# Gated mix of sliding-window attention and a SwiGLU feed-forward: a third gate/up tile computed as block products, and the dealing of the remaining slots

## The chip, the core and the metric

The kernel runs on one core of a Trainium2 chip. A core has five engines that work side by side and wait for each other through semaphores: TensorE (PE in the profile, its weight loads PEld), VectorE (DVE), ScalarE (ACT), GpSimd (POOL), and SyncE (SP), which here only issues transfers. The metric is the device time of one launch in microseconds. Times of repeated runs of this kernel lie within 1.2 us of each other (824.19 to 825.39 us).

## The reference

With x of 2048 rows and 512 columns, everything in float32:

```python
def _A_ref(x, wqkv, wo):                      # 32 heads of 16, window 256
    qkv = (x @ wqkv).reshape(B, S, 3, H, Dh).transpose(2, 0, 3, 1, 4)
    scores = einsum("bhqd,bhkd->bhqk", q, k) * Dh ** -0.5
    mask = (i - j >= 0) & (i - j < 256)
    o = softmax(where(mask, scores, -1e9)) @ v
    return o.reshape(B, S, D) @ wo

def _B_ref(x, w_gate, w_up, w_down):          # hidden width 1792
    return (silu(x @ w_gate) * (x @ w_up)) @ w_down

g = sigmoid((x * gate_w).sum(-1, keepdims=True))
return g * _A_ref(x) + (1 - g) * _B_ref(x)
```

## The kernel before

Every float32 operand is split into a high part (a rounded copy, made on ACT) and a low part (the rest, a subtraction on DVE or POOL), and a product is three matmuls: high by high, high by low, low by high. A matmul streams 512 columns of x; the contraction of 512 is cut into four blocks of 128. So one 128 by 512 piece of `x @ w` costs 12 matmuls of 128 rows.

The hidden width is cut into NF = 14 tiles of 128. A tile f has a gate part and an up part, (f, 0) and (f, 1), each with four pieces of 512 rows of x. They are computed in one of two ways.

**Block products.** `product` (line 367) and the loop at lines 416 to 447 handle a pair of keys at once: the pairs of `PAIRS` (lines 151 and 152) are four pairs of query/key groups, then one pair (gate, up) for each tile f below NSF (line 106). The two by two scheme forms sums of weight blocks and of x blocks and takes 7 products in place of 8. Each product is 6 matmuls (line 381), for two halves `a` of x: 7 x 2 x 6 = 84 matmuls for a pair, where the plain way takes 2 x 4 x 12 = 96. ACT copies results out of PSUM (`copied`), DVE adds (`add_to`), and for a feed-forward pair `put_c` sends the eight results of 256 KB to DRAM (`raws`) through the SP queue. While one pair's products run, the next pair's weights are fetched (`pair_fetch`) and prepared (`op_a`, `op_sums`, `op_s`, `op_z`). The last pair of the list has the other branch of that loop: it fills constant rows, stacks the queries and keys of the first head group, and fetches the first plain weights.

**Slots.** The other tiles are in `UNITS` (line 107), 24 units here. `stream` (line 581) is a generator that yields one slot at a time. The first unit goes through `whole`, 48 slots of one matmul of 128 rows. The rest goes through `lanes` (line 525): a slot there is two matmuls of 64 rows each, one in the upper and one in the lower half of the array, so 12 slots finish one 128 by 512 piece. The lower half runs LAG = 18 slots behind the upper one. When a piece is finished, `copy_out` (line 508) has ACT copy it out of PSUM (the eviction, L511) and SP writes it to `raws` three ticks later. `soft` moves an eviction that would fall in the last two ticks before the values of a group to the tick of the values. After the four pieces of a unit, `prepare` (line 299) has ACT and POOL split the next weights and SP fetch the ones after them.

**The attention stage.** The heads are in G = 8 groups of four, NB = 16 blocks of 128 rows each, so the loop at line 809 has 128 steps t of four ticks `hd`. In a tick PE gets, in this order: one score block of the next group (`stage1`, L603; DVE adds the mask and takes the maximum, L605), one score block of the present group (`stage2`, L642; ACT takes the exponential, L644; POOL cuts the window's edges, L646 and L649), then so many slots as `DEAL` says (lines 805, 806, 828). Four steps make a group of 16 ticks; at its second tick the values of the four steps before it are formed (`av`, L664) and copied out (`evacuate`). This text numbers the ticks of such a group 0 to 15: ticks 0 to 3 are part 0, 4 to 7 part 1, and so on. `DEAL` gives (4, 10, 8, 8) slots for the four parts; part 0 is dealt 1, 1, 2, 0. In the last head group (the last 16 steps) it gives 8 to every part, `stage1` has nothing left, `stage2` issues two blocks in every second tick, and pieces of the next stage are begun (`tile_early`: an exponential on ACT, two DVE reciprocal chains, splits).

Each engine takes its instructions in the order of the program. PSUM has eight banks: `stage2` has two in turn (one of them is lent to the values at ticks 1 to 2), `stage1` three, the slots three. A `stage2` matmul therefore waits until the exponential of the block two before it has been read out of the same bank. Before the loop there are 64 ticks with three slots each (lines 690 to 710), in which the first group's `stage1` runs. After the loop come the down product, the output projection and the mix (line 846 on).

The slots add up as follows: 192 before the loop and 28 x 30 + 4 x 32 = 968 in it make 1160, of which the generator has 48 + 1110 = 1158.

Of the kernel before, what the change touches and what calls it, by code (L numbers as in the profile page):

```python
# [33 lines left out]
def gated_mix(ctx, tc, xT, xn, wqk, wv, wo, wgu, wd, gw, out):  # L34
# [52 lines left out]
    def run(gen, n=None):  # L87

        while n is None or n > 0:
            if next(gen, run) is run:  # L90
                break
            n = n and n - 1
# [10 lines left out]
    def weights_of(key):  # L103
        return wqk[key[1]] if key[0] == "p" else wgu[key[1], :, key[2]]

    NSF = 2
    UNITS = [("f", f, i) for f in range(NSF, NF) for i in range(2)]

    psum = ctx.enter_context(tc.tile_pool(name="psum", bufs=1, space=PSUM))
# [17 lines left out]
    def pair_fetch(keys):  # L127
        raw = wide.tile([P, 4, 2 * P], F32, name="rw")
        for i, key in enumerate(keys):
            nc.sync.dma_start(by_k(raw[:, 2 * i:2 * i + 2].rearrange("p a n -> p (a n)")), weights_of(key))  # L130
        return raw
# [19 lines left out]
    PAIRS = [(("p", g), ("p", g + 1)) for g in range(0, G, 2)]  # L151
    PAIRS += [(("f", f, 0), ("f", f, 1)) for f in range(NSF)]
    RW = {0: pair_fetch(PAIRS[0])}
# [315 lines left out]
    with ExitStack() as A:  # L469
# [121 lines left out]
        def stage1(g, qb):  # L591

            hf, b = divmod(qb, NB // 2)
            if b == 0:
                MX[g, hf] = sm.tile([P, 4, NB // 2], F32, name="mx")
            q0, k0 = qb * P, max(0, qb - 2) * P
            n = q0 + P - k0
            for hd in range(4):
                pr, j = divmod(hd, 2)
                r = slice(64 * j, 64 * j + 63)  # L600

                ps = bank("pd") if g == 0 and pr else bank("pc")
                nc.tensor.matmul(ps[:, :n], QT[g % 2][pr][r, q0:q0 + P], KT[g % 2][pr][r, k0:k0 + n],  # L603
                                 start=True, stop=True)
                mx = nc.vector.tensor_tensor_reduce(out=ps[:, :n], in0=ps[:, :n], in1=mask[:, 3 * P - n:],  # L605
                                                    scale=1.0, scalar=NEG, op0=ALU.add, op1=ALU.max,
                                                    accum_out=MX[g, hf][:, hd, b:b + 1])
                if g == 0:
                    BEHIND.append(mx)
                yield  # L610
# [191 lines left out]
            spread(4 * (16 * g + 9) + 3, 1, stack(g + 2, 0))  # L802
            spread(4 * (16 * g + 17) + 1, 1, stack(g + 2, 1))

        DEAL = [[[(hd + 1) * n // 4 - hd * n // 4 for hd in range(4)] for n in deal] for deal in ((4, 10, 8, 8), (8, 8, 8, 8))]
        DEAL[0][0] = 1, 1, 2, 0
        scores = chain(*(stage1(*divmod(b, NB)) for b in range(NB, G * NB)))
        run(scores, 1)
        for t in range(G * NB + 1):
# [7 lines left out]
            for hd in range(4):  # L817
# [9 lines left out]
                if t < G * NB:  # L827
                    run(steps, DEAL[t >= g7][part][hd])
                if hd == 1 and values:
# [205 lines left out]
```

## Time and profile before

| | us |
|---|---|
| runs: lowest, median, highest | 824.19, 825.08, 825.39 |
| the profiled execution: its time | 822.77 |
| its span, first to last instruction | 821.1 |
| block products of the six pairs (L381), first to last matmul | 53.9 to about 165 |
| slots of `lanes` (L564) | 177.9 to 616.9 |
| `stage2` (L642) | 216.8 to 616.5 |

The profile gives the busy time of each engine, the span in 40 slices, and groups of instructions by line. Its chain of waits is followed back from the last instruction to what released it. The timeline lists single instructions by start and duration; where several of one kind follow on each other it gives the time from the first start to the last end and their number. Matmuls are pipelined: a matmul of 512 columns is listed with some 0.39 us, while the next one starts about 0.22 us after it, so that starts and not durations tell the pace.

### The profile page before, as it was taken

How to read it: one execution, taken by the hardware profiler on the slowest of the kernel's cores; microseconds unless marked ns; L12 is line 12 of the kernel's file. 1: busy time of each engine (PE TensorE's matmuls, PEld its weight loads, DVE VectorE, ACT ScalarE, POOL GpSimd, SP SyncE). 2: the span in 40 equal slices, each digit the busy share in tenths (PEclk: the TensorE clock that was granted, in tenths of full speed). 3: DMA queues.
4: the chain of work that ended last, by engine and by line, in shares of the span. 5: the costliest groups of instructions: out<-in, count | busy, mean ns of one | idle time of the engine just before them, and what ended most of it. 6: DMA issues, size and time to landing. Idle time of an engine off the chain costs nothing.

```text
span 821.1 us, 20501 instructions
## 1 busy us (share of the span) xinstructions
PE 812.8 (99%) x7681; PEld 692.3 (84%) x7681; DVE 552.3 (67%) x1425; ACT 470.7 (57%) x956; POOL 401.6 (49%) x715
## 2 busy tenths in 40 slices
PE   8999999999999999999999999999999999999997
PEld 7888888878888889888898888888887888888886
DVE  5675554248878788888888887776576666554652
ACT  6465453311577767767777676776776563435341
POOL 5124442260366666767667576665883205442320
PEclk9999999999999999999999999999999999999999
DMA  8446666475625554565455655442659897767611
GB/s 291 158 153 249 238 231 231 141 250 188 219 90 189 191 177 160 185 212 198 162 177 169 210 186 158 142 159 93 210 194 346 273 300 212 270 224 224 215 52 51
DMA packets 80211, 159.70 MB, mean 194 GB/s; under 512 B 14960, under 2 KB 19440, under 8 KB 80112
## 3 DMA queue, kind: packets, MB, share of 16 engines
q1 hardware_dynamic: 68544, 127.44, 47.1%
q0 software_dynamic: 10992, 29.91, 11.1%
q8 instruction: 60, 0.98, 0.5%
q10 hardware_dynamic: 576, 1.05, 0.4%
q14 instruction: 39, 0.32, 0.1%
HBM read 93.32 MB, written 65.01 MB: 193 GB/s over the span
## 4 chain that ended last, share of the span: by engine, by line
PE 95%; DMA 2%; DVE 1%; ACT 1%; SPq 0%; issue 0%; DVEq 0%; ACTq 0%
PE pa L564 22%; PE pb L564 11%; PE pd L642 7%; PE pc L664 5%; PE pd L381 4%; PE pb L381 4%; PE pa L381 4%; PE pd L83 3%; PE pc L82 3%; PE pc L83 3%; PE pc L81 3%; PE pd L82 3%; PE pd L81 3%; PE pd L664 3%; PE pc L381 2%; PE pb L82 2%
## 5 line engine op out<-in xcount | busy, mean ns | idle before, releaser
L644 ACT ACTIVATE pt<-pd 128x384 f32<-128x384 f32 (+2 forms) x491 | 223.7, 474 | 48.3 <-PE pd L642 29.9
L605 DVE CUSTOM_DVE_ANT_0 pc<-pc,mask 128x384 f32<-128x384 f32 (+2 forms) x322 | 173.0, 547 | 26.9 <-PE pc L603 12.2
L642 PE MATMUL pd<-q,k 64*128 64x384 f32 (+2 forms) x491 | 166.7, 348 | 1.2 <-ACT pt L644 1.2
L564 PE MATMUL pa<-xlo,wh 64*128 64x512 f32 x492 | 167.7, 397 | 0.0
L564 PE MATMUL pa<-xhi,wl 64*128 64x512 f32 x492 | 167.3, 393 | 0.0
L564 PE MATMUL pa<-xhi,wh 64*128 64x512 f32 x492 | 166.5, 391 | 0.0
L646 POOL TENSOR_SCALAR_AFFINE_SELECT pt<-pt 128x256 f32<-128x256 f32 x256 | 110.1, 431 | 73.7 <-ACT pt L644 67.4
L642 PEld LDWEIGHTS pd<-q,k 64*128 64x128 f32 x491 | 90.8, 186 | 23.3 <-ACT pt L644 8.8
L603 PE MATMUL pc<-k,q 63*128 63x384 f32 (+2 forms) x322 | 107.0, 337 | 0.0
L564 PE MATMUL pb<-xlo,wh 64*128 64x512 f32 x244 | 97.0, 397 | 0.0
L564 PE MATMUL pb<-xhi,wl 64*128 64x512 f32 x244 | 95.8, 393 | 0.0
L564 PE MATMUL pb<-xhi,wh 64*128 64x512 f32 x244 | 95.2, 390 | 0.0
L649 POOL TENSOR_SCALAR_AFFINE_SELECT pt<-pt 128x256 f32<-128x256 f32 x224 | 94.5, 422 | 0.0
L605 DVE CUSTOM_DVE_ANT_0 pb<-pb,mask 128x384 f32<-128x384 f32 (+2 forms) x158 | 86.7, 549 | 8.7 <-PE pb L603 5.4
L564 PEld LDWEIGHTS pa<-xhi,wh 64*128 64x128 f32 x492 | 87.8, 185 | 1.9 <-DVE mx L605 0.5
L564 PEld LDWEIGHTS pa<-xhi,wl 64*128 64x128 f32 x492 | 88.3, 185 | 1.3
L564 PEld LDWEIGHTS pa<-xlo,wh 64*128 64x128 f32 x492 | 86.7, 185 | 0.8
L605 DVE DVE_READ_ACCUMULATOR2_ANT mx<- 128x1 f32 x512 | 72.0, 141 | 0.0
L921 DVE TENSOR_TENSOR sg<-got,sg 128x512 f32<-128x512 f32 x52 | 41.1, 790 | 44.8 <-ACT sg L920 39.4
L664 PE MATMUL pd<-pt,vg 64*32 64x320 f32 (+4 forms) x1184 | 62.9, 346 | 0.0
L603 PEld LDWEIGHTS pc<-k,q 63*128 63x128 f32 x322 | 58.6, 184 | 5.0 <-issue 3.9
L682 POOL TENSOR_TENSOR oe<-oe,ob 128x512 f32<-128x512 f32 (+1 forms) x28 | 35.1, 1254 | 49.4 <-ACT ob L675 46.7
(307 smaller groups left out, 2064.3 us busy)
## 6 DMA issues: line engine op xcount, KB each, us to landing
got<-raws SPq DMA_DIRECT2D x104, 256.0 KB
raws<-ev SPq DMA_DIRECT2D x91, 256.0 KB
q<-xd SPq DMA_DIRECT2D x96, 128.0 KB
k<-xd SPq DMA_DIRECT2D x96, 128.0 KB
xd<-cx SPq DMA_DIRECT2D x16, 512.0 KB
xd<-cy SPq DMA_DIRECT2D x16, 512.0 KB
od<-oe POOLq DMA_DIRECT2D x32, 256.0 KB, 3.4
raw<-wgu SPq DMA_DIRECT2D x25, 256.0 KB
```

The lines of the kernel that those rows point to most:

```text
L81: nc.tensor.matmul(ps, lh, rh, start=start and i == 0, stop=False, skip_group_check=skip)
L82: nc.tensor.matmul(ps, lh, rl, start=False, stop=False, skip_group_check=skip)
L83: nc.tensor.matmul(ps, ll, rh, start=False, stop=stop and i == n - 1, skip_group_check=skip)
L381: nc.tensor.matmul(ps, l[:, w], r[:, k], start=n in (1, 2, 5) and k == m == 0, stop=k == 1 and m == 2, skip_group_check=True)
L564: mm = nc.tensor.matmul(ps[o], w[r], x[r], start=first and i == 0, stop=(o is odd or bool(lane)) and i == turn - 1)
L603: nc.tensor.matmul(ps[:, :n], QT[g % 2][pr][r, q0:q0 + P], KT[g % 2][pr][r, k0:k0 + n], start=True, stop=True)
L605: mx = nc.vector.tensor_tensor_reduce(out=ps[:, :n], in0=ps[:, :n], in1=mask[:, 3 * P - n:], scale=1.0, scalar=NEG, op0=ALU.add, op1=ALU.m ...
L642: nc.tensor.matmul(ps[:, :n], KT[g % 2][pr][r, k0:k0 + P], QT[g % 2][pr][r, k0:k0 + n], start=True, stop=True)
L644: BEHIND.append(nc.scalar.activation(pt[:, j, :n], ps[:, :n], AF.Exp, scale=SCALE))
L646: nc.gpsimd.affine_select(out=pt[:, :, :P], in_=pt[:, :, :P], pattern=[[0, 2], [1, P]], compare_op=ALU.is_ge, fill=0.0, base=0, channel_mu ...
L649: nc.gpsimd.affine_select(out=pt[:, :, 2 * P:], in_=pt[:, :, 2 * P:], pattern=[[0, 2], [-1, P]], compare_op=ALU.is_ge, fill=0.0, base=-1, ...
L664: nc.tensor.matmul(AV[g, c][h][32 * j:32 * j + 32, q0 - c * CH:q1 - c * CH], VG[4 * g + kb // 4][o, kb % 4, 17 * j:17 * j + 32], PT[g, kb, ...
```

## The change

```diff
-    NSF = 2
+    NSF = 3
     UNITS = [("f", f, i) for f in range(NSF, NF) for i in range(2)]
...
-        DEAL = [... for deal in ((4, 10, 8, 8), (8, 8, 8, 8))]
+        DEAL = [... for deal in ((4, 9, 7, 7), (8, 7, 7, 7))]
         DEAL[0][0] = 1, 1, 2, 0
```

`PAIRS` gets a seventh pair, the gate and up parts of tile 2. The former last pair (tile 1) goes through the loop's ordinary branch, and the new one through the last branch. `UNITS` loses two units and has 22: the slots needed are 48 + (83 x 12 + 18) = 1062. The dealing gives 192 + 28 x 27 + 4 x 29 = 1064. Within a part of n slots the four ticks get (hd + 1) n // 4 - hd n // 4: 9 is 2, 2, 2, 3 (10 was 2, 3, 2, 3), 7 is 1, 2, 2, 2 (8 was 2, 2, 2, 2). So the sixth tick of a group has two slots in place of three, and the first tick of part 2 and of part 3 has one in place of two.

More of the change, by code (lines that the diff above doesn't have):

```diff
@@ L803, in gated_mix @@
             spread(4 * (16 * g + 17) + 1, 1, stack(g + 2, 1))
-        DEAL = [[[(hd + 1) * n // 4 - hd * n // 4 for hd in range(4)] for n in deal] for deal in ((4, 10, 8, 8), (8, 8, 8, 8))]
+        DEAL = [[[(hd + 1) * n // 4 - hd * n // 4 for hd in range(4)] for n in deal] for deal in ((4, 9, 7, 7), (8, 7, 7, 7))]
         DEAL[0][0] = 1, 1, 2, 0
```

## The prediction

> **What bounds the kernel now.** I read the page first (engines, slices, chain), then the busy time by stretches, then single ticks of the attention stage, then the waits.
>
> ```profile
> span 821.1 us, 20501 instructions
> PE 812.8 (99%) x7681; PEld 692.3 (84%) x7681; DVE 552.3 (67%) x1425; ACT 470.7 (57%) x956; POOL 401.6 (49%) x715
> ...
> PE   8999999999999999999999999999999999999997
> ...
> ACT  6465453311577767767777676776776563435341
> ...
> PE 95%; DMA 2%; DVE 1%; ACT 1%; SPq 0%; issue 0%; DVEq 0%; ACTq 0%
> ```
>
> TensorE is busy in every slice and carries nearly all of the chain. Only TensorE work that disappears, or a wait in it, can move the end. The next view is the busy time of the engines in four stretches of 20 us (PE, PEld, DVE, ACT, POOL, each with its count).
>
> ```profile
> 120.00:140.00 20.00, 20.00 (x89) 16.55 (x89) 9.81 (x17) 8.75 (x15) 5.79 (x4) 1.00 0.66 235
> 140.00:160.00 20.00, 20.00 (x90) 16.56 (x89) 6.32 (x9) 6.05 (x10) 2.86 (x3) 1.00 0.45 156
> ...
> 440.00:460.00 20.00, 20.00 (x326) 16.98 (x322) 16.39 (x55) 14.21 (x31) 13.16 (x28) 1.00 0.47 154
> ...
> 600.00:620.00 20.00, 19.00 (x305) 15.04 (x303) 16.14 (x17) 16.13 (x39) 17.14 (x37) 1.00 0.55 191
> ```
>
> The first two rows are block products of feed-forward pairs: 90 matmuls in 20 us without a gap, the others half idle. The third is the attention stage: TensorE is called busy all the time, yet the other three are at 0.66 to 0.82. The fourth is the last head group, where TensorE does wait.
>
> **The pace of a tick.** In the attention stage the start of `stage1` (L603) marks a tick. These are TensorE's starts in one group; ticks 0 and 1 start at 442.36 and 442.76, ticks 7 to 13 from 449.30 to 453.41.
>
> ```profile
> 442.36 0.34 PE L603 MATMUL pc<-k,q 63*128 63x384 f32 x1
> 442.76 0.34 PE L603 MATMUL pb<-k,q 63*128 63x384 f32 x1
> ...
> 449.30 0.34 PE L603 MATMUL pc<-k,q 63*128 63x384 f32 x1
> ...
> 450.14 0.34 PE L603 MATMUL pc<-k,q 63*128 63x384 f32 x1
> ...
> 450.80 0.34 PE L603 MATMUL pb<-k,q 63*128 63x384 f32 x1
> ...
> 450.97 0.34 PE L642 MATMUL pd<-q,k 64*128 64x384 f32 x1
> ...
> 451.40 0.34 PE L603 MATMUL pc<-k,q 63*128 63x384 f32 x1
> ...
> 452.06 0.34 PE L603 MATMUL pc<-k,q 63*128 63x384 f32 x1
> ...
> 452.66 0.33 PE L603 MATMUL pb<-k,q 63*128 63x384 f32 x1
> 452.84 0.44 PE L642 MATMUL pd<-q,k 64*128 64x384 f32 x1
> ...
> 453.41 0.34 PE L603 MATMUL pc<-k,q 63*128 63x384 f32 x1
> ```
>
> One slot: 0.40 us (442.36 to 442.76). Three slots: 0.84 (449.30 to 450.14). Two slots: 0.66, 0.60, 0.66, 0.60, then 0.75 for tick 12 (452.66 to 453.41). A slot is worth about 0.22 us, the same as a full matmul of the products, and one of these ticks is 0.12 too long. ACT's rows beside it say why (exponentials L644, evictions L511):
>
> ```profile
> 450.75 1.09 ACT L644 ACTIVATE pt<-pd 128x384 f32<-128x384 f32 x2 [0.41 <-PE pd L642]
> 451.81 0.59 ACT L511 COPY ev<-pa 128x512 f32<-128x512 f32 x1
> 452.29 1.52 ACT L644 ACTIVATE pt<-pd 128x384 f32<-128x384 f32 x3
> ```
>
> ```profile
> L644 ACT ACTIVATE pt<-pd 128x384 f32<-128x384 f32 x430 | 204.0, 494 | 42.4 <-PE pd L642 24.7 <-POOL pt L649 0.6 <-PE pa L564 0.3
> ```
>
> The exponential of tick 9 (the second of the first row) is followed by an eviction, which holds ACT until the exponential of tick 10 can start at 452.29. That one lasts 0.49 (the last row, a group of 430), and at 452.84 the `stage2` block of tick 12 starts, as it needs the bank of tick 10. So from the `stage2` of tick 9 (450.97) to that of tick 12 an eviction needs 1.87 us, and three ticks of two slots last 1.86: no room is left, and the tick loses some 0.1. The wait hides in "20.00 busy". The wait view for the weight loads between 217 and 567 us counts such waits, and is a lower bound, since it sees only what is left after the load before:
>
> ```profile
> PEld pd L642 <- ACT pt L644: 5.7, 26, 0.4
> PEld pd L642 <- ACT ob L675: 5.1, 26, 0.2
> ```
>
> **The change, part by part.** The sum is made against the profiled execution, 822.77 us (span 821.1 and 1.7 around it); the median of the runs, 825.08, stands 2.3 above it, and I add the difference to the median.
>
> *The seventh pair.* 84 matmuls at 20.00/90 = 0.222 us: **+18.7** (18.9 by the row with 89). Its copies, sums, splits and eight 256 KB writes lie under the products, as they do for the pair in the row of 120 to 140 us, where DVE has 9.81, ACT 8.75 and DMA 0.66 of the time; two feed-forward pairs follow each other today already. The SP queue takes the same eight writes and two weight fetches out of the attention stage, so nothing queues behind more than before. Without this cover (were each copy waited for) PE would not show 20.00 there.
>
> *The slots.* 96 go: 28 groups lose three, the four groups of the last heads lose three each. At 0.222 the first 84 are **-18.7**, the last 12 **-2.7**. So the bare TensorE work gained is 96 - 84 = 12 matmuls, 2.7 us. All else depends on whether the shorter ticks are really shorter.
>
> *Evictions that meet the one-slot ticks.* A piece ends every 12 slots. With 30 slots a group, evictions fell on five places of a cycle of two groups (ticks 4, 9, 1 and 7, 12 after the shift of `soft`); two of the five, at ticks 9 and 12, met three two-slot ticks and cost about 0.1 each: 0.1 per group. With 27 slots there are nine places in four groups: after slots 2, 5, 8, 11, 14, 17, 20, 23 and 26 of a group, which are ticks 2, 4, 6, 7, 9, 10, 12, 14 and 15 (the last moved to 1). For each I compare the three ticks behind it with 1.87 + 0.1:
> Ticks 4 and 1: room enough, 0. Ticks 6 and 7: a three-slot and a one-slot tick are among the three, 1.84 to 1.88 us, and behind 9 stand three of two slots, 1.86: about 0.1 each. Ticks 10 and 12: two two-slot ticks and one one-slot tick, 0.60 + 0.63 + 0.40 = 1.63 to 1.66, so 0.33 each. Tick 14: its late exponential meets the values, which wait for ACT anyway, 0.05. Tick 2 is new and falls right behind the values, where ACT is late already. The trace has that case with a weight split (L69) in the eviction's place:
>
> ```profile
> 484.72 0.62 ACT L69 CAST wh<-raw 128x512 fp32r<-128x512 f32 x1
> 485.23 1.52 ACT L644 ACTIVATE pt<-pd 128x384 f32<-128x384 f32 x3
> ```
>
> ```profile
> 485.46 0.33 PE L603 MATMUL pc<-k,q 63*128 63x384 f32 x1
> ...
> 486.60 0.33 PE L603 MATMUL pb<-k,q 63*128 63x384 f32 x1
> ```
>
> Tick 5 there takes 1.14 us for three slots, 0.30 more than 0.84. Summed over four groups: 3 x 0.1 + 2 x 0.33 + 0.05 + 0.30 = 1.31, or 0.33 per group, less 0.1 of today, plus 0.02 for the weight splits, one in 48 slots, on the same places: 0.25 x 28 = **+7.0**. Bounds: at best today's waits go as well (0.1 x 28: -2.8); at worst both one-slot ticks of every group save nothing (2 x 0.222 x 28: +12.4). I stay at 7.0, since its prices are rows of the same stage, not of a far one.
>
> The Trainium skill speaks against this change: its page "Trainium Kernel Development and Optimization", section "Best Practices", says to mind PSUM pressure, as tiling speeds up TensorE but not the emptying of PSUM. The rows above agree for tick 12. By that rule alone the one-slot ticks would be worth nothing, and by the slot's pace alone they would be worth all; the former is the third rival below.
>
> *The last head group.* ACT, DVE and POOL are at 16 to 17 of 20 there. The chain of waits runs through DVE and ACT in the last group of ticks:
>
> ```profile
> 606.46 2.50 PE pc L664 x95
> ...
> 609.66 0.69 DVE oe L677
> ...
> 610.72 3.36 DVE ev L750
> ...
> 615.68 0.62 ACT q L69
> 616.53 0.33 PE pd L642
> ...
> 617.26 2.64 PE pc L664 x91
> ```
>
> ```profile
> ACT q L69 <- DVE ev L752: 1.0, 1, 1.0
> ```
>
> From the values of t = 124 on, the sum of the attention output (L677), a reciprocal of 3.36 us and a split set the last exponentials and the last values; ACT stands a full 1.0 us for it. TensorE's slots are no part of it, so the last three removed ones return nothing (0.67 us). For the other nine I count on about two thirds, as ACT is behind there for stretches: 1.4 of 2.7 is lost: **+1.4** (0 to 2.7).
>
> Sum: 18.7 - 18.7 - 2.7 + 7.0 + 1.4 = +5.7. Profiled 828.5, median 825.08 + 5.7 = **830.8 us**.
>
> Costed at nothing: DVE has 16.39 of 20 us and would come to 0.85 of a group of 12.1 us (12.55 today: 32 issues of `od` from 232.6 to 621.5, below), POOL to 0.68; without that cover a DVE wait would cost what it lacks per tick. The lower lane's start waits for the exponential behind the upper lane's end, six slots later; one-slot ticks put more time between them, not less. Transfers: 0.47 of the engines.
>
> ```profile
> L683 POOL DMA_DIRECT2D od<-oe x32: 540/557/584, 232.6 to 621.5; - x32
> ```
>
> **The rivals.**
>
> 1. *The full saving, on the other side.* The queue of matmuls and the skew of the two lanes swallow ACT's lateness, as they do today for 1.86 against 1.87. Then only the last group's chain costs: -2.7 + 0.7 = -2.0, or -2.7 if that goes too: 822.4 to 823.1. It decides once the waits are below 0.07 us per group. For it: ACT is at only 14.21 of 20. Against: tick 12 pays already, with a slot more.
> 2. *Break-even.* Evictions behind ticks 10 and 12 cost only what their slot saved, the one behind tick 2 nothing: about 2 x 0.22 + 0.3 in four groups, less 0.1 a group, 0.085 x 28 = 2.4; with +1.4 and -2.7 that is +1.1: 826.2.
> 3. *ACT's pace rules parts 2 and 3.* Every one-slot tick is followed by a wait, eviction or not (exponential 0.37 behind its block, 0.49 long, 0.06 to the next: 0.92 against 0.40 + 0.60 in two ticks, only 0.08 of room). Then only the slots of part 1 count: +18.7 - 6.2 - 1.3 = +11.2: 836.3. The rule of the Trainium skill named above would have it so.
> 4. *The new pair isn't covered* (its weights or `raws` writes come late): some 1 to 3 us on top, 832 to 834. Against it: the row of 120 to 140 us.
>
> **How the numbers follow.** Forecast 0.52, rival 1 0.13, rival 2 0.15, rival 3 0.12, rival 4 0.08. What a measurement of this kernel can tell from no change is about 0.2%, 1.65 us. Faster by more is rival 1 and the low end of 2: 0.14. Within it, most of rival 2: 0.12. Slower: 0.74. The forecast's own range is 827.5 to 833.5; to hold eight in ten I take 823 to 835, which leaves out the ends of rivals 1 and 3.
>
> **What would show it.** The added pair: L381 with 588 matmuls at 0.222 us, PE at 20.00 of 20. The slots: 2/3-slot ticks as now, one-slot ticks at 0.40 except three ticks behind an eviction. The waits: L642's waits on L644 well above 5.7 us, groups of ticks, by the issues of `od`, at about 12.1 us (12.55 - 0.67 + 0.25), not 11.9 (rival 1) or 12.3 (rival 3). The last group: the last values still about 10.8 us behind those before (606.46 to 617.26). The prediction is wrong if groups last under 12.0 us or if the product stage grows by other than 18.7.

## The result and the profile after

The changed kernel takes 830.78 us (median of 5 runs, 830.16 to 831.3), the kernel before 825.08 (5 runs, 823.27 to 826.95): a ratio of 1.0081, interval 1.0065 to 1.0098. The change makes the kernel slower, by 5.7 us of median. Between the two profiled executions the difference is larger: span 829.0 against 821.1, +7.9, since the one of before was 2.3 below the median of its runs and the one of after lies on its own.

The page of the changed kernel, its span and engines:

```profile
span 829.0 us, 20299 instructions
PE 819.7 (99%) x7573; PEld 681.8 (82%) x7573; DVE 553.6 (67%) x1438; ACT 469.1 (57%) x957; POOL 399.2 (48%) x713
```

TensorE has 108 matmuls fewer (7573 against 7681) and is busy 6.9 us longer, still at 99%. Busy time at 99% tells little of waits here: a matmul of 512 columns is listed with 0.39 us while the next one starts 0.22 us after it, so a start that is up to 0.17 us late leaves no idle time in this sum. The busy time by stretches (PE, PEld, DVE, ACT, POOL):

```profile
120.00:140.00 20.00, 20.00 (x90) 16.57 (x89) 9.82 (x17) 8.73 (x15) 5.78 (x4) 1.00 0.64 228
...
460.00:480.00 20.00, 20.00 (x257) 17.17 (x256) 17.23 (x62) 14.80 (x35) 14.23 (x31) 1.00 0.71 225
```

The block products run as before (90 matmuls in 20 us), and in the attention stage, the second row, TensorE again shows 20.00 of 20, although its listed waits there are almost three times what they were, as will be seen. Where the first 128-row slot starts tells what the new pair costs; lines of before and of after, with first and last start:

```profile
L518 PE MATMUL pa<-xhi,wh x8: 389/389/390, 165.4 to 170.2; 128*128 128x512 f32 x8
```

```profile
L518 PE MATMUL pa<-xhi,wh x8: 389/389/389, 184.1 to 188.9; 128*128 128x512 f32 x8
```

165.4 to 184.1: +18.7, and the added pair hides all its copies, sums and writes. The groups of the attention stage by the issues of `od`, and the waits of `stage2` on the exponentials between 235 and 575 us (217 to 567 before):

```profile
L683 POOL DMA_DIRECT2D od<-oe x32: 542/560/584, 251.1 to 630.2; - x32
```

```profile
PEld pd L642 <- ACT pt L644: 15.4, 51, 0.7
```

(630.2 - 251.1) / 31 = 12.23 us a group, after 12.55. The listed waits on the exponentials rise from 5.7 to 15.4 us.

**Where the time went.** Cut by the starts of the matmuls, the +7.9 of the two profiles is: block products +18.73; 27 groups from the first tick 0 to the last, 12.601 to 12.226 each, -10.14; from there to the values of t = 112, +0.14; from these values to the end of the last ones, 49.10 to 49.02, -0.08; the rest, 201.20 to 200.47, -0.73.

The groups can be cut further. Mean time of each tick from one start of `stage1` to the next, 26 groups (the first, shorter one left out), us:

| tick | 0 | 1 | 2 | 3 | 4 | 5 | 6 | 7 | 8 | 9 | 10 | 11 | 12 | 13 | 14 | 15 | sum |
|---|---|---|---|---|---|---|---|---|---|---|---|---|---|---|---|---|---|
| before | .39 | 3.03 | .58 | .34 | .87 | .90 | .63 | .85 | .64 | .61 | .64 | .61 | .69 | .62 | .64 | .65 | 12.68 |
| after | .38 | 3.10 | .58 | .35 | .89 | .72 | .63 | .89 | .39 | .66 | .66 | .64 | .40 | .72 | .64 | .66 | 12.30 |

The three ticks that lost a slot (5, 8, 12) are shorter by 0.18, 0.25 and 0.29, 0.72 in all, which is more than 3 x 0.222: tick 12 also lost its old wait. Of this, 0.34 comes back in the others: tick 13 +0.10, tick 1 +0.06, tick 9 +0.05, tick 7 +0.04, the rest 0.03 or less each. Two examples. First, an eviction behind tick 10; the starts of ticks 11 to 14 (L603) with the `stage2` block of tick 13, and ACT beside them:

```profile
439.73 0.34 PE L603 MATMUL pc<-k,q 63*128 63x384 f32 x1
...
440.36 0.34 PE L603 MATMUL pc<-k,q 63*128 63x384 f32 x1
...
440.78 0.33 PE L603 MATMUL pb<-k,q 63*128 63x384 f32 x1
441.12 0.44 PE L642 MATMUL pd<-q,k 64*128 64x384 f32 x1
...
441.70 0.34 PE L603 MATMUL pc<-k,q 63*128 63x384 f32 x1
```

```profile
439.63 0.49 ACT L644 ACTIVATE pt<-pd 128x384 f32<-128x384 f32 x1
440.09 0.59 ACT L511 COPY ev<-pa 128x512 f32<-128x512 f32 x1
440.58 1.52 ACT L644 ACTIVATE pt<-pd 128x384 f32<-128x384 f32 x3
```

The one-slot tick 12 lasts 0.42. Tick 13 lasts 0.92 where two slots take 0.63: its `stage2` block needs the bank of tick 11, whose exponential stood behind the eviction and ran from 440.58 to about 441.08; the block starts at 441.12, 0.34 after the tick in place of 0.18. Second, an eviction at tick 2, right behind the copies of the values (L675); ticks 3 to 6:

```profile
446.58 0.34 PE L603 MATMUL pc<-k,q 63*128 63x384 f32 x1
...
446.95 0.44 PE L603 MATMUL pc<-k,q 63*128 63x384 f32 x1
...
447.23 0.43 PE L642 MATMUL pd<-q,k 64*128 64x384 f32 x1
...
447.79 0.33 PE L603 MATMUL pb<-k,q 63*128 63x384 f32 x1
448.10 0.44 PE L642 MATMUL pd<-q,k 64*128 64x384 f32 x1
...
448.69 0.34 PE L603 MATMUL pc<-k,q 63*128 63x384 f32 x1
```

```profile
446.25 0.54 ACT L675 COPY ob<-pd 128x448 f32<-128x448 f32 x1 [1.79 <-PE pc L664]
446.68 0.50 ACT L644 ACTIVATE pt<-pd 128x384 f32<-128x384 f32 x1
447.06 0.60 ACT L511 COPY ev<-pa 128x512 f32<-128x512 f32 x1
447.52 0.90 ACT L644 ACTIVATE pt<-pd 128x384 f32<-128x384 f32 x2
```

Tick 5 (447.79 to 448.69) takes 0.90 for two slots: its block waits until 448.10 for the exponential of tick 3. Tick 4 (446.95 to 447.79) takes 0.84 for two slots, and about as long in the kernel before (0.87 in the table): its block, at 447.23, waits for the exponential of tick 2, which stands behind the copy of the values and ends at about 447.18. Tick 3, with no slot, is so short that this wait shows.

### The profile page after: what moved, and what is told of

It is laid out like the page before. It is cut to its first block, busy times and chain, and to the rows that moved or that the text cites. A ratio compares the mean times of both kernels' runs of the same rounds, so it can differ in the third digit from the quotient of the medians.

```text
span 829.0 us, 20299 instructions
## 1 busy us (share of the span) xinstructions
PE 819.7 (99%) x7573; PEld 681.8 (82%) x7573; DVE 553.6 (67%) x1438; ACT 469.1 (57%) x957; POOL 399.2 (48%) x713
## 4 chain that ended last, share of the span: by engine, by line
PE 96%; ACT 1%; DVE 1%; DMA 1%; issue 0%; POOL 0%; DVEq 0%; SPq 0%; ACTq 0%
PE pa L564 20%; PE pb L564 10%; PE pd L642 7%; PE pc L664 5%; PE pd L381 5%; PE pb L381 5%; PE pa L381 5%; PE pd L81 3%; PE pc L83 3%; PE pd L83 3%; PE pd L82 3%; PE pc L82 3%; PE pc L81 3%; PE pd L664 3%; PE pc L381 2%; PE pb L83 2%
## 5 line engine op out<-in xcount | busy, mean ns | idle before, releaser
L644 ACT ACTIVATE pt<-pd 128x384 f32<-128x384 f32 (+2 forms) x491 | 220.4, 476 | 43.0 <-PE pd L642 21.5
L564 PE MATMUL pa<-xhi,wl 64*128 64x512 f32 x448 | 155.6, 398 | 0.0
L564 PE MATMUL pa<-xlo,wh 64*128 64x512 f32 x448 | 153.5, 399 | 0.0
L564 PE MATMUL pa<-xhi,wh 64*128 64x512 f32 x448 | 150.8, 394 | 0.0
L646 POOL TENSOR_SCALAR_AFFINE_SELECT pt<-pt 128x256 f32<-128x256 f32 x256 | 110.3, 431 | 67.4 <-ACT pt L644 63.8
L603 PE MATMUL pc<-k,q 63*128 63x384 f32 (+2 forms) x322 | 107.0, 337 | 0.0
L564 PE MATMUL pb<-xlo,wh 64*128 64x512 f32 x224 | 89.6, 400 | 0.0
L564 PE MATMUL pb<-xhi,wl 64*128 64x512 f32 x224 | 88.7, 396 | 0.0
L564 PE MATMUL pb<-xhi,wh 64*128 64x512 f32 x224 | 88.6, 396 | 0.0
L564 PEld LDWEIGHTS pa<-xhi,wl 64*128 64x128 f32 x448 | 80.2, 185 | 0.8
L564 PEld LDWEIGHTS pa<-xhi,wh 64*128 64x128 f32 x448 | 79.1, 185 | 1.6 <-DVE mx L605 0.5
L564 PEld LDWEIGHTS pa<-xlo,wh 64*128 64x128 f32 x448 | 78.5, 185 | 0.5
L603 PEld LDWEIGHTS pc<-k,q 63*128 63x128 f32 x322 | 58.6, 184 | 5.0 <-issue 4.3
```

Source lines behind the costliest of these rows:

```text
L564: mm = nc.tensor.matmul(ps[o], w[r], x[r], start=first and i == 0, stop=(o is odd or bool(lane)) and i == turn - 1)
L644: BEHIND.append(nc.scalar.activation(pt[:, j, :n], ps[:, :n], AF.Exp, scale=SCALE))
L646: nc.gpsimd.affine_select(out=pt[:, :, :P], in_=pt[:, :, :P], pattern=[[0, 2], [1, P]], compare_op=ALU.is_ge, fill=0.0, base=0, channel_mu ...
```

## The experiments

Groups are given as the mean of 27, from the first tick 0 to the last; the last head group from the values of t = 112 to the end of the last values.

**1. A slot moved under the wait of tick 4.** Tick 3 gets one slot, in the changed kernel from tick 7, in the kernel before from tick 5. First the edit of the changed kernel, then that of the kernel before.

```diff
-    ... for deal in ((4, 9, 7, 7), (8, 7, 7, 7))]
-    DEAL[0][0] = 1, 1, 2, 0
+    ... for deal in ((5, 8, 7, 7), (8, 7, 7, 7))]
+    DEAL[0][0] = 1, 1, 2, 1
```

```diff
-    ... for deal in ((4, 10, 8, 8), (8, 8, 8, 8))]
-    DEAL[0][0] = 1, 1, 2, 0
+    ... for deal in ((5, 9, 8, 8), (8, 8, 8, 8))]
+    DEAL[0][0] = 1, 1, 2, 1
```

> The changed kernel with one slot moved from tick 7 (three slots, now two) to tick 3 (none, now one) of every group with 27 slots. Theory: tick 4 lasts 0.87 us for two slots, 0.24 more than such a tick needs, because its stage2 block waits for ACT's exponential of tick 2, which is late behind the values. A slot at tick 3 runs inside that wait and costs nothing, while tick 7 gets 0.22 us shorter: groups 12.23 to about 12.01 us, the whole about 6 us faster than the changed kernel, 824 to 826 us. Rival: ticks are paced by TensorE alone, so that a slot costs 0.22 us wherever it stands: groups stay at 12.23 and the time at 830.8.

> The kernel before with the same move: tick 3 gets one slot, tick 7 two in place of three (30 slots a group as before, two tiles as block products). Theory: groups 12.60 to about 12.38 us, the whole 6 us under the kernel before, about 819 us. Rival: no difference, 825.

| tick | 3 | 4 | 5 | 7 | 8 | 10 | group (27) |
|---|---|---|---|---|---|---|---|
| before | .34 | .87 | .90 | .85 | .64 | .64 | 12.601 |
| before, slot moved | .60 | .64 | .67 | .89 | .62 | .62 | 12.415 |
| after | .35 | .89 | .72 | .89 | .39 | .66 | 12.226 |
| after, slot moved | .60 | .66 | .72 | .65 | .43 | .72 | 12.092 |

(A part of 10 slots has its three-slot ticks at 5 and 7, one of 9 at 7 alone.) In both kernels tick 3 grows by 0.25 to 0.26 and tick 4 shrinks by 0.23 to 0.24 without any change of its own slots: the moved slot runs in time that was a wait. (For the kernel before, the expectation names tick 7 as the one that loses the slot; by the dealing it is tick 5.) The kernel before becomes 818.22 us (ratio 0.9939, 0.9917 to 0.996, beside 824.35 of the kernel before in these runs), as expected. The changed kernel becomes 826.8 (1.0034, 1.0019 to 1.0048). Its groups gain 0.134, not 0.22: ticks 10 and 8 grow by 0.06 and 0.03, where an eviction now stands ahead of shorter ticks, and tick 0 by 0.05, most of it one tick 1.2 us longer than usual, whose cause is open. The waits on the exponentials do not fall there:

```profile
PEld pd L642 <- ACT pt L644: 17.0, 56, 0.6
```

So a slot has no fixed price. It costs 0.22 where TensorE is the bound and next to nothing where a wait would be.

**2. The evictions at ticks 10 and 2 moved.** Changed kernel; those at tick 10 go to DVE, those at tick 2 come two ticks later.

```diff
-    soft(0, lambda: nc.scalar.copy(place, ps))
+    tick = NOW[0] % 16 if 0 <= NOW[0] < 4 * (G - 1) * NB else None
+    if tick == 10: later(0, lambda: nc.vector.tensor_copy(place, ps))
+    elif tick == 2: later(2, lambda: nc.scalar.copy(place, ps))
+    else: soft(0, lambda: nc.scalar.copy(place, ps))
```

> The changed kernel; in the seven head groups with stage1 the evictions that fall on tick 10 run on DVE in place of ACT, and those on tick 2 are issued two ticks later. Theory: the wait of tick 13 (0.92 us there, 0.63 elsewhere) and that of tick 5 (0.88 against 0.63) go, as ACT's exponential is no longer late: 0.29 + 0.25 in four groups, groups 12.23 to about 12.09 us, the whole 3 to 4 us less than the changed kernel, if DVE has the room (it is at 0.86). Rival: the long ticks come from the order of slots in the two lanes, not from ACT: they stay, 0.

827.21 us (one run); groups 12.097, -0.129. Tick 5 falls from .72 to .65, tick 13 from .72 to .65, the other ticks stay within 0.03. The waits of `stage2` (its lines are six higher here):

```profile
PEld pd L648 <- ACT pt L650: 9.4, 36, 0.7
```

15.4 to 9.4, 51 to 36: this is the cause of the two lost ticks. The two places together are worth 0.129 x 27 = 3.5 us.

**3. A third bank for `stage2`.** If the wait is one for a bank, a third one takes it away. It is taken from `stage1`.

```diff
     BANKS["pa"].remove("pb1")
-    BANKS["pc"].append("pb1")
+    BANKS["pd"].append("pb1")
...
-    if t == g7:
-        BANKS["pc"].remove("pb1")
-        BANKS["pd"].append("pb1")
```

> The changed kernel with the eighth PSUM bank given to stage2 from the start (three banks in turn) and taken from stage1 (two). Theory: stage2's waits for the exponentials, 15.4 us in 51 waits in the changed kernel between 235 and 575 us, nearly go (under 4 us), the ticks 4, 5, 10 and 13 lose their excess; stage1 then waits for DVE in their place, 0.2 to 0.5 us a group behind the values, so that groups come out between 11.9 and 12.4 us. Rival (not the bank, the lanes): waits and groups as they are, 12.23.

841.95 us (one run); groups 12.590, above the 11.9 to 12.4 expected. The waits of `stage2` on the exponentials are gone from the list of the weight loads, and these have come:

```profile
PEld pc L603 <- DVE mx L605: 9.2, 37, 1.1
...
PEld pc L603 <- DVE oe L681: 7.6, 27, 0.3
```

Tick 4 is .64 (from .89) and tick 13 .60 (from .72), so the bank was what both waited for, though the ticks ahead of them are longer here too and give ACT more time. Tick 5 does not get shorter: behind an eviction at tick 2 its median falls from .88 to .76, but in two of the three other kinds of groups it rises from .64 to .75. But `stage1` with two banks waits for DVE: tick 2 .91 (from .58), tick 11 .78 (from .64), tick 14 .76 (from .64). Eight banks don't feed both.

**4. The old dealing in the changed kernel.** The groups take 84 slots more than in the changed kernel, so the slots run out early and the last head group has 30 in place of 114. (`put_back` fetches a piece that waits in DRAM; it comes earlier for that.)

```diff
-    at(4 * (g7 + 8), put_back)
+    at(4 * g7, put_back)
...
-    ... for deal in ((4, 9, 7, 7), (8, 7, 7, 7))]
+    ... for deal in ((4, 10, 8, 8), (8, 8, 8, 8))]
```

> Three tiles as block products, but the slots dealt as before (30 a group): they run out some four steps into the last head group, whose other twelve steps have none (the partial piece kept in DRAM is read back eight steps earlier for that). Theory: the groups are those of the kernel before, 12.60 us, 18.7 us later; the last head group, 49 us in both kernels, is set by DVE's and ACT's chain and not by TensorE's slots, so that 84 slots fewer leave it at 37 us or more. Rival: TensorE's slots set it, 49 - 84 x 0.222 = 30 us.

838.94 us (one run); groups 12.613, those of the kernel before (12.601), so the gain of the groups comes from the dealing, not from the pair in front. The last head group still takes 46.70 us, only 2.3 less than 49.02, though 84 slots, 18.7 us of TensorE, are gone from it. TensorE's slots don't set its length, though part of it ran at a lower clock (see the end).

**5. What sets the last head group.** The chain of waits of the changed kernel through its last ticks (start, us, engine and line):

```profile
617.08 0.60 ACT ev L511
617.68 0.68 DVE oe L677
618.36 0.34 DVE ev L749
...
618.73 3.37 DVE ev L750
...
624.83 0.95 DVE den L458
625.78 0.28 issue
626.06 0.50 POOL rd L460
...
626.62 0.55 POOL raws L512
...
627.18 0.43 POOL pt L646
...
627.65 0.32 PE pc L664 x8
```

The reciprocal of 3.37 us, a second one (L458), a write that POOL issues only once that is done (L460), another issue, and then the last window cut (L646), for which the last values wait. Three edits, each in the changed kernel: the addition of L749 given to ACT; the write of the second reciprocal issued five ticks later; the addition on ACT and, besides, the raw weights (L796) and the last unit's pieces (L510) issued by SP.

```diff
-    lambda: nc.vector.tensor_scalar(sg, sg, 1.0, None, op0=ALU.add),
+    lambda: nc.scalar.activation(sg, sg, AF.Copy, bias=1.0),
```

```diff
-    for n in (0, 8, 11):
+    for n in (0, 8, 16 if c else 11):
```

```diff
-    queue = nc.gpsimd if key == UNITS[-1] else nc.sync
+    queue = nc.sync
...
-    nc.gpsimd.dma_start(WDRAW[f], wd[f])
+    nc.sync.dma_start(WDRAW[f], wd[f])
```

> The changed kernel with the two additions of 1 in the early pieces (the tensor_scalar on DVE, 2.77 us for the first of them in the changed kernel and 0.56 before) made on ACT. Theory: that instruction waits for POOL, whose instructions stand back to back there, and DVE's chain behind it sets the last values; without it the first reciprocal starts 2 us earlier, ACT's wait of 1.4 us for the second one and POOL's of 1.7 us for DVE go, and the last head group falls from 49.0 to about 47 us, the whole to about 829 us. Rival: ACT and TensorE set the last head group, which stays at 49 or gets 0.5 longer by ACT's two additions.

> The changed kernel with the last write of the reciprocal sums on the POOL queue issued behind the last edge cuts in place of ahead of them. Theory: the last values (3.45 us against 2.68 before) wait for POOL's last cuts, which stand behind that write, which waits 1.7 us for DVE; without it they take 2.7 us, and the whole falls by about 0.7 us. Rival: the last exponentials are late by themselves; nothing changes.

> The kernel after with the addition of L749 on ACT, as in the run before it, and with two kinds of transfers issued by SP instead of POOL: the raw weights of the last tiles of the down product (L796, three issues) and the pieces of the last unit (L510). If POOL's queue sets the end of the last head group (its last window selects stood behind such issues, and the last values took 4.25 us instead of 3.45): the last values take about 3 us, the time from the values of t = 112 to the end of the last values falls from 49.67 to 48 or 48.5, and the run is 1.2 to 1.7 below 831.45, about 830. Rival, the issues cost POOL nothing or SP is late with them: 49.5 or more, 831 to 832.

The first two gave nothing, against what was expected: 831.45 us with a last head group of 49.67, and 831.83 with 49.70 (one run each). With the addition on ACT the first reciprocal starts 1.2 us earlier (611.39 against 612.63), but the last window cuts do not; POOL in that run:

```profile
623.37 0.56 POOL L796 DMA_DIRECT2D raw<-wd  x1
623.93 0.54 POOL L796 DMA_DIRECT2D wh<-wd  x1
...
625.95 0.56 POOL L460 DMA_DIRECT2D rd<-den  x1
626.50 0.55 POOL L512 DMA_DIRECT2D raws<-ev  x1
627.06 1.30 POOL L646 TENSOR_SCALAR_AFFINE_SELECT pt<-pt 128x256 f32<-128x256 f32 x2
```

Five issues of 0.55 us, three of them L796, stand close ahead of two cuts. With four of them moved to SP, POOL has

```profile
625.46 0.56 POOL L460 DMA_DIRECT2D rd<-den  x1 [0.89 <-DVE den L458]
626.03 0.77 POOL L646 TENSOR_SCALAR_AFFINE_SELECT pt<-pt 128x256 f32<-128x256 f32 x2
```

and the last values take 2.56 us in place of 4.25, the last head group 47.92 in place of 49.67, as expected. POOL's queue was the bound there. Yet the run takes 834.18 us (4 runs; ratio 1.0141, 1.0116 to 1.0167), 4 above what was expected: the time behind the last values grows from 200.8 to 203.8 us. SP and ACT say why:

```profile
619.21 0.38 SPq L796 DMA_DIRECT2D raw<-wd  x1
623.30 0.33 SPq L796 DMA_DIRECT2D wh<-wd  x1
...
624.20 0.85 SPq L743 DMA_DIRECT2D k<-raws  x2
```

```profile
629.11 0.63 ACT L760 ACTIVATE ev<-k 128x512 f32<-128x512 f32 x1
629.65 0.57 ACT L675 COPY ob<-pc 128x512 f32<-128x512 f32 x1
```

SP stops for 3.7 us between two of the weight fetches, and the fetch of the next tile (L743, at 615.92 without the edit) is queued behind them. ACT's activation of that tile waits for it, and behind this one stands the copy of the last values: 629.65, 2.05 us after they end (0.05 without the edit). A wait on POOL has become one on SP and ACT.

**6. The best version.** The kernel before with the slot moved (experiment 1), the addition on ACT and the later write of the reciprocal; then the same with the issues moved to SP.

> Two tiles as block products, a slot moved from tick 7 to tick 3, the additions of 1 on ACT and the last write of the reciprocal sums behind the cuts. Theory: the former gives 6 us (818.2 measured with it alone, whose last head group took 51.5 us, 2.4 more than before, as its tensor_scalar took 3.35 us); the other two bring that last head group to about 48.5 us: 815 to 816 us. Rival (DVE's chain doesn't matter): 818.

> The fastest kernel so far (the kernel before with tick 3 given a slot of tick 7, the addition on ACT and the last write of the reciprocals five ticks later, 816.99) with the same two kinds of transfers issued by SP. If POOL's queue sets the end of the last head group there: 49.56 falls by about 1, 816. Rival: no change, 817, or more if SP is late.

The first takes **816.99 us** (4 runs; ratio 0.9924, 0.9908 to 0.9941, beside 823.39), faster than both kernels. In the profiled executions its last head group takes 49.56 (48.5 was expected), against 51.52 in experiment 1's kernel. But the latter execution was the slowest of five of its kernel (820.71, the others 817.62 to 818.65), and beside the kernel before the two ratios, 0.9924 and 0.9939, lie within each other's intervals: that the two edits pay is not shown, and the moved slot alone gives nearly all of the gain. The second takes 820.12 (0.9963, 0.9949 to 0.9978), where 816 was expected: the last head group falls to 48.93, but the time behind it grows from 201.2 to 204.7.

## Why the prediction was right

830.8 us were forecast and 830.78 measured, but not every term stands, and the closeness is partly chance.

*The seventh pair:* +18.7 forecast, +18.73 measured. Rival 4 (not covered) falls.

*The shorter groups:* -18.7 + 7.0 = -11.7 forecast for 28 groups, -10.14 + 0.14 = -10.0 measured. The mechanism is the one forecast: evictions ahead of one-slot ticks make `stage2` wait for a bank (experiments 2 and 3). By 12.601 - 0.667 the bare slots would give 11.93 (rival 1), and rival 3 gives 12.38; measured are 12.226, so the net wait is 0.29 per group, where 0.25 was forecast. The figure of "about 12.1" for the group was off by another 0.05, since its base of 12.55 counted the shorter last head group (49.10 / 4 = 12.3) with the others.

*The places.* The evictions fall on the ticks forecast. By medians of the tick three behind each: behind tick 10 +0.29 (forecast 0.33), behind 2 +0.25 (0.30), behind 7 +0.10 and behind 6 +0.07 (0.1 each), behind 9 nothing (0.1), behind 4 +0.09 (0). Behind 14 it is the tick of the values that grows: tick 1 of the next group takes 3.36 against 3.21, +0.15 (0.05). The mis-sized place is tick 12: tick 15 loses nothing where 0.33 was forecast. The prediction took every block to be 384 columns wide. Four groups of 16 ticks make a head group, so an eviction at tick 12 always falls in the last of the four, in the last step, where `stage2` has 128 columns left: the exponential behind the eviction takes 0.28 us in place of 0.49 and ends at 331.13 in one such group, ahead of the weight load of tick 15's block at 331.21. The places add up to 0.95 in four groups, 0.24 each, where 0.33 was forecast. Single long ticks hide that: nine ticks in the 26 groups are over 0.15 longer than the median of their place, together 0.10 per group (three, 0.03, in the kernel before), six of them one or two ticks behind a weight split (L69), for which 0.02 was forecast. Rival 2, which had tick 2 free, falls; rival 3, a wait behind every one-slot tick, falls too, since ticks 8 and 12 last .39 and .40 and their successors lose only where an eviction is near. The rule of the Trainium skill named beside it in the prediction (page "Trainium Kernel Development and Optimization", section "Best Practices": mind PSUM pressure) thus holds for banks behind an eviction, and experiment 3 shows that PSUM is indeed the limit, but it did not make every one-slot tick worthless.

*The last head group:* -2.7 + 1.4 = -1.3 forecast, -0.08 measured. This term was mis-sized: the whole of the 2.7 is lost, not half. Experiment 4 shows why: the group's length hardly depends on the slots. The last values follow the ones before after 11.1 us (10.8 forecast).

*The rest:* the -0.73 behind the last values was not forecast, and no run explains it.

Measured terms add up to 18.73 - 10.0 - 0.08 - 0.73 = +7.9 against a forecast of +5.7. That the time agrees comes from the 2.3 us between the profiled execution of before and the median of its runs; in later runs the kernel before had medians of 824.35, 823.39 and 823.23. The changed kernel was not run again beside these, so its size is known only as 5.7 to some 7.5 us.

## What to carry to other kernels

A piece of filler work on the bound engine is free only under a wait, so read the starts tick by tick to find the ticks that are longer than their work, and put it there: one slot moved to such a tick makes the kernel before 6 us faster, while three slots less in each group bring back little more than half of their time (0.375 of 0.667 us). Before shortening a tick, check which slower consumer (here ACT, by an exponential plus an eviction) has to hand back a buffer within it. Before moving a transfer to another queue, see what stands behind it there.

## What the runs showed of the hardware

An addition on DVE (L749) took 0.42 and 0.56 us in the kernel before, but one of the two took 2.77 in the changed kernel and 3.35 in the kernel before with the slot moved. The row of the kernel before (lowest, median and highest duration in ns), those of the other two, then POOL's of the changed one at that time:

```profile
L749 DVE TENSOR_SCALAR ev<-ev x2: 417/488/560, 602.0 to 610.3; 128x512 f32<-128x512 f32 x2
```

```profile
609.83 2.77 DVE L749 TENSOR_SCALAR ev<-ev 128x512 f32<-128x512 f32 x1 [0.28 <-ACT ev L748]
```

```profile
596.53 3.35 DVE L749 TENSOR_SCALAR ev<-ev 128x512 f32<-128x512 f32 x1 [0.34 <-ACT ev L748]
```

```profile
609.96 1.29 POOL L72 TENSOR_TENSOR wl<-raw,wh 128x512 fp32r<-128x512 f32 x1
...
612.28 0.58 POOL L649 TENSOR_SCALAR_AFFINE_SELECT pt<-pt 128x256 f32<-128x256 f32 x1
```

POOL works without a gap from 609.22 on; the addition ends only at 612.60, when one of POOL's cuts, usually 0.41, takes 0.58. In four other runs of the changed kernel with edits (experiments 1, 2, 3 and the later write) it took 2.76 to 2.78. This looks like DVE waiting for something that POOL holds, over several of POOL's instructions. The Trainium skill, page "SBUF — State Buffer", section "Who interferes with whom", says that the two share a pair of ports under an exclusive lock, and names `tensor_scalar` among the operations that can contend. The trace agrees in kind; a wait over a whole row of POOL's instructions is more than the blocking by one. No run isolates it, though with the addition on ACT the reciprocal behind it does start 1.2 us earlier.

In experiment 4, where TensorE had little work left, its granted clock fell. Stretches of 4 us, the clock being the number ahead of the last two:

```profile
604.00:608.00 4.00, 4.00 (x11) 2.37 (x11) 3.30 (x6) 3.99 (x11) 3.99 (x8) 0.64 0.98 330
608.00:612.00 4.00, 4.00 (x59) 1.84 (x66) 1.68 (x3) 1.55 (x4) 4.00 (x9) 0.51 0.80 225
```

In the changed kernel, with its slots, it is 1.00 in every 4 us from 600 to 628 us. So the 46.70 us of experiment 4 hold some time at a lower clock and are no clean bound for the other engines. That the slots keep the clock up fits the two runs; none isolates it.
